# Memory attention and a SiLU feed-forward on one core: weights in order of use, lower parts on GpSimd, folded gates, two buffers for a head's operands

## The chip, the core and the metric

The kernel runs on one core of a Trainium2 chip. The core has a matrix engine (PE, whose weight loads PEld run beside its products), a vector engine (DVE), a scalar engine (ACT), GpSimd (POOL) and a queue, SP, that issues transfers. Each engine takes its instructions in a fixed order, and an instruction that waits holds up everything behind it on that engine. The metric is the device time of one execution in microseconds (us).

## What is computed

```python
# attention with a memory, B=8, H=8, S=576, D=64
scores = where(causal, -1e9, q @ k.T / sqrt(D))
a = exp(scores - scores.max(-1));  a /= a.sum(-1) + 1e-9
local = a @ v
q_p = where(q > 0, q, exp(q) - 1) + 1
mem_out = (q_p @ M_prev) / (q_p @ z_prev + 1e-6)
g = 1 / (1 + exp(-beta))                     # one number per head
x = g * mem_out + (1 - g) * local            # 8*576 tokens x 512
# feed-forward on x: w_in 512 x 2048, w_out 2048 x 512 (given as float64)
h = x @ w_in;  out = (h * sigmoid(h)) @ w_out
```

## The kernel before, in words

**Two kinds of work.** There are 64 heads of attention (8 per batch entry), and a feed-forward of 18 units of 256 tokens, each of 8 steps (p = 0 to 7). A step makes 24 products into a PSUM tile `h` (line 548), turns it into `g` (lines 559 to 564), and makes 12 products into `acc` (line 528). All products but those of the first heads take operands split into a rounded part and a lower part (fp32r), so that a product is made of two or three products at full rate. The first `N_WHOLE` heads take fp32 operands instead ("whole"), which needs no split but more PE time.

**A head** has two generators. `scores` transposes q and k (`tt`), makes the rounded parts (`kk`, `qq`, on ACT) and the lower parts (`kk`, `ql`, `qq`, lines 229 and 232, on DVE), then five blocks of scores: minimum on DVE (260, 291), exponential on ACT with a row sum (262, 296). The last block is laid out as two halves (`pair`) of 64 partitions; one of its halves gets the causal mask by an addition on GpSimd (284). `scale_rows` turns row sums into 1/(sum) on DVE, and GpSimd scales the probabilities by it and by 1 - g (250). `values` transposes the probabilities on PE, splits them (405, 406) and multiplies them with v and the memory (413, 421). `values` of a head runs beside `scores` of the next one.

**Weights** arrive as 64-bit words. `split_weight` decodes one of 32 tiles with two ACT, three DVE and one POOL instructions and splits it with one ACT and one POOL instruction (lines 149 to 161). Twelve of the tiles (`FLOW`) don't stay on chip: they are written to scratch through two `flow` buffers, and read again through the same two buffers in every unit (`flow()`, line 481). In the kernel before, the list `order` holds the twelve FLOW tiles first.

**What sets the order.** The main loop draws steps from three generators: one step of attention, then weights, then feed-forward steps at `FFN_RATE` once `done[0]`, the number of finished heads, is at least 8. `done[0]` counts a head after the next head's `scores` too. From that program a scheduler makes the order of each engine, using buffer counts (`QK_BUFS`, `NB`, `TH_BUFS`, ...) as limits.

Of the kernel before, what the change touches and what calls it, by code (L numbers as in the profile page):

```python
# [34 lines left out]
PREP_FROM = 8  # L35
PREP_REST = 100
# [7 lines left out]
def memory_attention_then_silu_ffn(ctx, tc, q, k, v, M_prev, z_prev, beta, w_in, w_out, out):  # L44
    nc = tc.nc
# [30 lines left out]
    def f(ap):  # L76
# [13 lines left out]
        compare_op=ALU.is_ge, fill=BIG,  # L90
    )
    gate = const.tile([P, H], F32, name="gate")
    omg = const.tile([P, H], F32, name="omg")
    nc.sync.dma_start(out=gate, in_=beta.rearrange("(o h) -> o h", o=1).to_broadcast([P, H]))
    nc.scalar.activation(gate, gate, AF.Exp, scale=-1.0)
    nc.vector.tensor_scalar(gate, gate, 1.0, None, op0=ALU.add)
    nc.vector.reciprocal(gate, gate)
    nc.vector.tensor_scalar(omg, gate, -1.0, 1.0, op0=ALU.mult, op1=ALU.add)
# [41 lines left out]
    def split_weight(kind, c, raw):  # L140
        t = weight_tile(kind, c)
        w = raw
        if raw.dtype == I64:
            words = raw.bitcast(U32).rearrange("p (n t) -> p n t", t=2)
            low, high = words[:, :, 0], words[:, :, 1]
            y = pool.tile([P, DM], U32, tag="wy", name="wy", bufs=W_BUFS)
# [20 lines left out]
    order = [(kind, 2 * p + j) for p in range(NP) for kind in "io" for j in range(2)]  # L167
    order.sort(key=lambda x: x not in FLOW)
# [43 lines left out]
    def scores(b, h, raw, rest, made, whole):  # L212
# [6 lines left out]
        if whole:  # L219
            qq = pool.tile([P, S], F32, tag="kk", name="qf", bufs=QK_BUFS)  # L220
            nc.scalar.activation(qq[0:64], tt[64:P], AF.Copy, scale=QS)
            terms = [(qq[0:64], tt[0:64])]
        else:
            kk = pool.tile([P, S], F32R, tag="kk", name="kk", bufs=QK_BUFS)
            qq = qrow[h % QK_BUFS]
            ql = qlow[h % QK_BUFS]
            nc.scalar.copy(kk[0:64], tt[0:64])
            nc.scalar.activation(qq[64:P, 0:S], tt[64:P], AF.Copy, scale=QS)
            nc.vector.tensor_tensor(out=kk[64:P], in0=tt[0:64], in1=f(kk[0:64]), op=ALU.subtract)
            nc.scalar.activation(qq[0:64, 0:S], tt[64:P], AF.Copy, scale=QS)  # L230
            for low, x0, x1 in ((ql[0:64], 0, S - LAST), (qq[0:64, S:S + LAST], S - LAST, S)):
                nc.vector.scalar_tensor_tensor(
                    out=low, in0=tt[64:P, x0:x1], scalar=QS, in1=f(qq[64:P, x0:x1]),
                    op0=ALU.mult, op1=ALU.subtract)
            nc.scalar.copy(qq[:, S + LAST:], f(qq[:, S - LAST:S]))
            terms = [(qq, kk), (ql, kk)]
# [5 lines left out]

        def scale_rows(n, i0, i1):
            s, r = st[0:n, 10 + i0:10 + i1], st[0:n, 15 + i0:15 + i1]
            nc.vector.tensor_scalar(s, s, 1.0e-9, None, op0=ALU.add)
            nc.vector.reciprocal(r, s)  # L246
            if n == LAST:
                nc.vector.tensor_copy(st[n:P, 15 + i0:15 + i1], r)
            for i in range(i0, i1):
                nc.gpsimd.tensor_scalar(  # L250
                    pb[i], pb[i], st[:, 15 + i:16 + i], omg[:, h:h + 1], op0=ALU.mult, op1=ALU.mult)

        for i in range(NQ - 1):
# [3 lines left out]
            for j, (ta, tb) in enumerate(terms):  # L257
# [3 lines left out]
                s, s, mask[:, 3 * P - P * i:], 1.0, 3.0e38, ALU.add, ALU.min, st[:, i:i + 1]).ins  # L261
# [10 lines left out]
        for side, other, x0, x1, o in ((slice(0, LAST), slice(LAST, P), 0, SPLIT, P),  # L272
                                       (slice(LAST, P), slice(0, LAST), SPLIT, S, 0)):
            s = ps_s.tile([P, 512], F32, tag="s", name="s")[:, 0:x1 - x0]
# [15 lines left out]
        for s, row, more, least in halves:  # L290
            nc.vector.tensor_tensor_reduce(row, s, more, 1.0, 3.0e38, ALU.add, ALU.min, least)
        up, down = slice(0, LAST), slice(LAST, P)
        nc.vector.tensor_copy(st[up, 6:7], st[down, 5:6])
        nc.vector.tensor_tensor(out=st[up, i:i + 1], in0=st[up, 5:6], in1=st[up, 6:7], op=ALU.min)
        anchor["dve"] = nc.vector.tensor_copy(st[down, i:i + 1], st[up, i:i + 1]).ins
        nc.scalar.activation(
            pt, pair, AF.Exp, bias=st[:, i:i + 1], scale=-1.0, accum_out=st[:, 10 + i:11 + i])
        pb.append(pt)
        scale_rows(P, 0, NQ - 1)
        yield  # L300
        nc.vector.tensor_copy(st[up, 7:8], st[down, 10 + i:11 + i])
        nc.vector.tensor_tensor(
            out=st[up, 10 + i:11 + i], in0=st[up, 10 + i:11 + i], in1=st[up, 7:8], op=ALU.add)
        scale_rows(LAST, NQ - 1, NQ)
        if not whole:
            nc.gpsimd.tensor_copy(pt[down, HI:], pt[down, HI - LAST:HI])
# [128 lines left out]
    def attention():  # L435
# [12 lines left out]
        for n in range(len(todo) + 1):  # L448
# [14 lines left out]
            done[0] = n  # L463
# [45 lines left out]
    def ffn():  # L509
        ahead = None  # L510
        for _ in range(FLOW_BUFS):
            flow()
        for u in range(NU):
# [7 lines left out]
            def second(p, g):  # L521
                for c in range(2):
# [8 lines left out]
                    if ("o", 2 * p + c) in FLOW:  # L531
                        flow()

            before = None
            for p in range(NP):
# [6 lines left out]
                for c in range(2):  # L542
# [39 lines left out]
    steps, prepared, produced, steps_made = 0, 0, 0.0, 0
# [48 lines left out]
```

## Time and profile before

| | |
|---|---|
| median of 3 runs | 1349.75 us (1349.42 to 1352.28) |
| profiled execution, its own time | 1345.04 us |
| its span in the profile | 1343.3 us |
| PE busy | 1279.5 us (95%) |
| DVE busy | 1047.2 us (78%) |
| ACT busy | 799.9 us (60%) |
| POOL busy | 661.0 us (49%) |

Busy times are averages over stages that differ: the first heads with the weights (to about 204 us), attention and feed-forward side by side (to about 1140 us), and feed-forward alone. The span is 1.7 us shorter than the execution's own time.

### The profile page before, as it was taken

To read this page: it belongs to the slowest core of one execution; us is meant where nothing else is said; L and a number is where in the kernel's file an instruction comes from. 1 tells how busy PE (TensorE), PEld (TensorE's weight loads), DVE (VectorE), ACT (ScalarE), POOL (GpSimd) and SP (SyncE) were. 2 spreads that over 40 slices of the span, in tenths; PEclk is the share of its full clock that TensorE was granted. 3 is DMA by queue.
4 is the path that set the end of the run, shared out by engine and by line. 5 is a ranking of instruction groups with operands and counts; after the bars stand their busy time and mean duration, and the time that the engine had idled before them with its cause. 6 is when DMAs were issued, how large, how long until landed. Compare 5 with 4: busy or idle time off the path is not lost.

```text
span 1343.3 us, 24742 instructions
## 1 busy us (share of the span) xinstructions
PE 1279.5 (95%) x7863; PEld 1089.2 (81%) x7863; DVE 1047.2 (78%) x2918; ACT 799.9 (60%) x1994; POOL 661.0 (49%) x985
## 2 busy tenths in 40 slices
PE   6999899999999999999899999999999989999998
PEld 2444357998889898989899898989998888899997
DVE  7878996889999889998889888999989888322222
ACT  6766775667667566766666665767766665211111
POOL 5768894555545454555545555555555544111110
PEclk9965799999999999999999999999999999999999
DMA  7865535556455454555454545555555542344444
GB/s 170 233 172 168 138 109 127 150 126 162 123 136 149 119 153 128 146 136 135 130 145 121 160 124 139 146 138 136 150 148 134 136 124 79 126 143 156 157 157 141
DMA packets 302994, 190.39 MB, mean 142 GB/s; under 512 B 258832, under 2 KB 267024, under 8 KB 302864
## 3 DMA queue, kind: packets, MB, share of 16 engines
q1 hardware_dynamic: 302864, 188.82, 51.7%
q8 instruction: 62, 1.02, 0.3%
q14 instruction: 68, 0.56, 0.1%
HBM read 173.02 MB, written 15.73 MB: 141 GB/s over the span
## 4 chain that ended last, share of the span: by engine, by line
PE 68%; DVE 18%; ACT 4%; DMA 3%; POOL 3%; issue 3%; SPq 1%; DVEq 0%; POOLq 0%; ACTq 0%
PE h L548 26%; PE acc L528 22%; PE x L421 7%; PE s L258 5%; PE tp L375 4%; DVE xu L501 1%; DVE th L560 1%; DMA flow<-wo_s 1%; DVE pl L406 1%; DVE tt L218 1%; DVE s L260 1%; DVE qp L358 1%; PE x L413 1%; POOL p L250 1%; DVE e L326 1%
## 5 line engine op out<-in xcount | busy, mean ns | idle before, releaser
L548 PE MATMUL h<-xu,wi 128*128 128x256 f32 x2592 | 381.3, 290 | 30.4 <-DVE th L560 23.1
L548 PEld LDWEIGHTS h<-xu,wi 128*128 128x128 f32 x2592 | 348.6, 195 | 46.6 <-DVE th L560 28.7
L250 POOL TENSOR_SCALAR p<-p,st,omg 128x384 f32<-128x384 f32 (+3 forms) x320 | 232.1, 737 | 109.0 <-DVE st L246 42.4
L528 PE MATMUL acc<-wo,g 128*128 128x512 f32 x864 | 245.6, 400 | 0.5 <-DVE g L564 0.5
L528 PE MATMUL acc<-flow,g 128*128 128x512 f32 x864 | 237.8, 398 | 2.4 <-DMA flow<-wo_s 2.4
L563 POOL TENSOR_SCALAR g<-th 128x512 fp32r<-128x512 f32 x144 | 90.7, 630 | 291.5 <-DVE th L560 269.2
L262 ACT ACTIVATE p<-s,st 128x128 f32<-128x128 f32 (+3 forms) x256 | 134.9, 527 | 125.7 <-DVE st L260 109.6
L560 DVE SCALAR_TENSOR_TENSOR th<-th,h 128x512 f32<-128x512 f32 x144 | 98.4, 684 | 113.6 <-ACT th L559 111.8
L528 PEld LDWEIGHTS acc<-flow,g 128*128 128x128 f32 x864 | 157.1, 188 | 34.5 <-DMA flow<-wo_s 4.1
L528 PEld LDWEIGHTS acc<-wo,g 128*128 128x128 f32 x864 | 151.2, 189 | 22.4 <-DVE g L564 0.9
L559 ACT ACTIVATE th<-h 128x512 f32<-128x512 f32 x144 | 85.2, 592 | 129.9 <-PE h L548 129.5
L260 DVE CUSTOM_DVE_ANT_0 s<-s,mask 128x128 f32<-128x128 f32 (+3 forms) x256 | 123.6, 496 | 21.9 <-PE s L258 20.3
L564 DVE TENSOR_TENSOR g<-th,g 128x512 fp32r<-128x512 f32 x144 | 107.8, 749 | 35.3 <-POOL g L563 33.6
L548 PE MATMUL h<-xu,flow 128*128 128x256 f32 x864 | 130.2, 286 | 0.5 <-DMA flow<-wi_s 0.5
L327 POOL TENSOR_TENSOR r<-e,zb 128x320 f32<-128x320 f32 x64 | 58.2, 910 | 142.5 <-DVE e L326 127.5
L375 PE MATMUL tp<-ident,p 128*128 128x128 f32 x640 | 121.3, 289 | 2.5 <-POOL flow L161 1.5
L406 DVE TENSOR_TENSOR pl<-tp,ph 128x384 fp32r<-128x384 f32 x212 | 114.7, 551 | 9.4 <-ACT ph L405 6.3
L548 PEld LDWEIGHTS h<-xu,flow 128*128 128x128 f32 x864 | 114.3, 191 | 0.9 <-DMA flow<-wi_s 0.7
L405 ACT CAST ph<-tp 128x384 fp32r<-128x384 f32 x212 | 101.2, 490 | 23.1 <-PE tp L383 18.5
L375 PEld LDWEIGHTS tp<-ident,p 128*128 128x128 f32 x640 | 80.1, 146 | 24.9 <-issue 12.2
L421 PE MATMUL x<-ph,vs 128*128 128x320 f32 (+4 forms) x371 | 83.8, 280 | 0.2 <-POOL vs L315 0.2
L421 PE MATMUL x<-pl,vs 128*128 128x320 f32 (+3 forms) x318 | 79.9, 305 | 2.0 <-DVE pl L406 2.0
(106 smaller groups left out, 2346.1 us busy)
## 6 DMA issues: line engine op xcount, KB each, us to landing
flow<-wo_s SPq DMA_DIRECT2D x144, 512.0 KB, 3.5
flow<-wi_s SPq DMA_DIRECT2D x72, 512.0 KB, 4.0
raw<-in_k SPq DMA_DIRECT2D x128, 72.0 KB, 2.9
raw<-in_q SPq DMA_DIRECT2D x128, 72.0 KB, 2.9
out<-o SPq DMA_DIRECT2D x36, 256.0 KB, 4.2
wraw<-in_moe_w_out SPq DMA_DIRECT2D x16, 512.0 KB, 5.2
qn<-in_q SPq DMA_DIRECT2D x64, 128.0 KB, 3.7
vr<-in_v SPq DMA_DIRECT2D x64, 128.0 KB, 3.0
```

Of the source, the lines that this page charges most:

```text
L250: nc.gpsimd.tensor_scalar(pb[i], pb[i], st[:, 15 + i:16 + i], omg[:, h:h + 1], op0=ALU.mult, op1=ALU.mult)
L260: anchor["dve"] = nc.vector.tensor_tensor_reduce(s, s, mask[:, 3 * P - P * i:], 1.0, 3.0e38, ALU.add, ALU.min, st[:, i:i + 1]).ins
L262: nc.scalar.activation(pt, s, AF.Exp, bias=st[:, i:i + 1], scale=-1.0, accum_out=st[:, 10 + i:11 + i])
L375: nc.tensor.transpose(t[:, o:o + P], pb[i][:, P * j:P * j + P], ident)
L405: nc.scalar.copy(ph[:, 0:o], t[:, 0:o])
L406: nc.vector.tensor_tensor(out=pl[:, 0:cut], in0=t[:, 0:cut], in1=f(ph[:, 0:cut]), op=ALU.subtract)
L421: nc.tensor.matmul(x[0:rows, q0:n], vs[0:n_k, j], part[0:n_k, o:o + n - q0], start=False, stop=last)
L528: nc.tensor.matmul(acc[t], ta, tb, start=p == 0 and c == 0 and n == 0, stop=p == NP - 1 and c == 1 and n == len(terms) - 1)
L548: nc.tensor.matmul(h[:, c], ta, tb, start=kk == 0 and n == 0, stop=kk == KD - 1 and n == len(terms) - 1)
L560: nc.vector.scalar_tensor_tensor(out=th, in0=th, scalar=1.0, in1=h, op0=ALU.add, op1=ALU.mult)
L563: nc.gpsimd.tensor_scalar(hi, th, 1.0, 1.0, op0=ALU.mult, op1=ALU.mult)
L564: nc.vector.tensor_tensor(out=lo, in0=th, in1=f(hi), op=ALU.subtract)
```

## The change

Six things change. (1) The list `order` of weights follows their use, resident and FLOW tiles mixed, and they are made at one rate (`PREP_RATE`) instead of 2.5 per nine steps and then all at once. (2) Feed-forward steps may begin as soon as `values` of the eighth head is done, `flow()` waits until its weight is ready, and a step that asks for a weight no longer uses up the allowance of the feed-forward. (3) The lower parts `kk`, `ql`, `qq` go from DVE to GpSimd; the scale of q by -1/8 goes from them into the minimum's instruction. (4) The gates g and 1 - g are folded into the two denominators as `over` (1 + exp(-beta) and 1 + exp(beta)), so that GpSimd scales with one operand column instead of two, and all five scalings of a head come after the last block's sum. (5) `kk`, `qq`, `ql`, `tt` get two buffers; to make room, `th`, `o` and `wy` share four `row` buffers. (6) `N_WHOLE` goes from 11 to 10, so that the eleventh head is split.

```diff
-TH_BUFS = 2
-QK_BUFS = 1
+QK_BUFS = 2
-NB = dict(vs=1, e=2, r=1, qp=1, ms=2, raw=1, qn=2, mr=3, zb=2, st=2, nrm=2, ph=2, pl=2, xb=1, tt=1)
+NB = dict(vs=1, e=2, r=1, qp=1, ms=2, raw=1, qn=2, mr=3, zb=2, st=2, nrm=2, ph=2, pl=2, xb=1, tt=2)
-N_WHOLE = 11
-O_BUFS = 2
-W_BUFS = 4
+N_WHOLE = 10
+ROW_BUFS = 4
-PREP_FLOW = 2.5
-PREP_FROM = 8
-PREP_REST = 100
+PREP_RATE = 3.0
+PREP_AFTER = 3.0
...
+    nc.scalar.activation(bet[:, 0], bet[:, 0], AF.Exp, scale=-1.0)
+    nc.scalar.activation(bet[:, 1], bet[:, 1], AF.Exp)
+    nc.vector.tensor_scalar(bet, bet, 1.0, None, op0=ALU.add)
+    over = const.tile([P, 2, H, NQ], F32, name="over")
+    for j in range(2):
+        for hh in range(H):
+            nc.gpsimd.tensor_scalar(over[:, j, hh], mask[:, 0:NQ], bet[:, j, hh:hh + 1], None, op0=ALU.add)
...
-    order = [(kind, 2 * p + j) for p in range(NP) for kind in "io" for j in range(2)]
-    order.sort(key=lambda x: x not in FLOW)
+    order = [
+        (kind, 2 * x + j) for p in range(NP + 1) for kind, x in (("i", p), ("o", p - 1))
+        if 0 <= x < NP for j in range(2)]
...
-            nc.scalar.activation(qq[64:P, 0:S], tt[64:P], AF.Copy, scale=QS)
-            nc.vector.tensor_tensor(out=kk[64:P], in0=tt[0:64], in1=f(kk[0:64]), op=ALU.subtract)
-            nc.scalar.activation(qq[0:64, 0:S], tt[64:P], AF.Copy, scale=QS)
+            nc.scalar.copy(qq[64:P, 0:S], tt[64:P])
+            nc.gpsimd.tensor_tensor(out=kk[64:P], in0=tt[0:64], in1=f(kk[0:64]), op=ALU.subtract)
+            nc.scalar.copy(qq[0:64, 0:S], tt[64:P])
             for low, x0, x1 in ((ql[0:64], 0, S - LAST), (qq[0:64, S:S + LAST], S - LAST, S)):
-                nc.vector.scalar_tensor_tensor(
-                    out=low, in0=tt[64:P, x0:x1], scalar=QS, in1=f(qq[64:P, x0:x1]),
-                    op0=ALU.mult, op1=ALU.subtract)
+                nc.gpsimd.tensor_tensor(
+                    out=low, in0=tt[64:P, x0:x1], in1=f(qq[64:P, x0:x1]), op=ALU.subtract)
...
-        scale_rows(P, 0, NQ - 1)
         yield
-        nc.vector.tensor_copy(st[up, 7:8], st[down, 10 + i:11 + i])
-        nc.vector.tensor_tensor(
-            out=st[up, 10 + i:11 + i], in0=st[up, 10 + i:11 + i], in1=st[up, 7:8], op=ALU.add)
-        scale_rows(LAST, NQ - 1, NQ)
+        halves_of(10 + i, 6, ALU.add)
+        nc.vector.scalar_tensor_tensor(
+            out=st[:, 15:15 + NQ], in0=st[:, 10:10 + NQ], scalar=1.0e-9, in1=over[:, 1, h],
+            op0=ALU.add, op1=ALU.mult)
+        nc.vector.reciprocal(st[:, 15:15 + NQ], st[:, 15:15 + NQ])
+        for x in range(NQ):
+            nc.gpsimd.tensor_scalar(
+                pb[x], pb[x], st[:, 15 + x:16 + x], 1.0, op0=ALU.mult, op1=ALU.mult)
...
-        nc.vector.tensor_scalar(nrm, nrm, 1.0e-6, None, op0=ALU.add)
+        nc.vector.scalar_tensor_tensor(
+            out=nrm, in0=nrm, scalar=1.0e-6, in1=over[:, 0, h], op0=ALU.add, op1=ALU.mult)
         nc.vector.reciprocal(nrm, nrm)
-        nc.vector.tensor_scalar(nrm, nrm, gate[:, h:h + 1], None, op0=ALU.mult)
...
-                two = two and next(second, "end") != "end"
+                if two and next(second, "end") == "end":
+                    two = False
+                    done[0] = n
...
-            done[0] = n
...
         if flow_order:
+            while flow_order[0] not in ready:
+                yield "prepare"
             x = flow_order.pop(0)
...
-        while going and prepared < 2 * KF and prepared < (
-                PREP_FLOW * min(steps, H * A_STEPS) + PREP_REST * max(steps - PREP_FROM * A_STEPS, 0)) / A_STEPS:
+        started = done[0] >= H
+        while going and len(ready) < min(2 * KF, steps * (PREP_AFTER if started else PREP_RATE) / A_STEPS):
             next(prep)
```

**GpSimd, one head in the middle of the run.** `g` is the feed-forward's rounding, `p_...` are the probabilities, `pair` the mask addition, `r` and `e` the memory's normalization, `vs` and `ms` operands of the values. Before:

```order
L250 TENSOR_SCALAR p_9446<-p_9446,st,omg 128x128
L250 TENSOR_SCALAR p_9488<-p_9488,st,omg 128x256
L250 TENSOR_SCALAR p_9507<-p_9507,st,omg 128x384
L250 TENSOR_SCALAR p_9543<-p_9543,st,omg 128x512
L284 TENSOR_TENSOR pair<-pair,mask 64x64
L317 TENSOR_SCALAR ms<-mr 128x64
L318 TENSOR_TENSOR ms<-mr,ms 128x64
L327 TENSOR_TENSOR r<-e,zb 128x320
L563 TENSOR_SCALAR g<-th 128x512
```

The same engine after the change, from the end of one head's scalings:

```order
L304 TENSOR_SCALAR p_11558<-p_11558,st 128x384
L307 COPY p_11558<-p_11558 64x64
L318 TENSOR_SCALAR ms<-mr 128x64
L319 TENSOR_TENSOR ms<-mr,ms 128x64
L235 TENSOR_TENSOR ql_155<-tt,qq_151 64x512
L235 TENSOR_TENSOR qq_151<-tt,qq_151 64x64
L277 TENSOR_TENSOR pair<-pair,mask 64x64
L328 TENSOR_TENSOR r<-e,zb 128x320
L232 TENSOR_TENSOR kk<-tt,kk 64x576
L315 TENSOR_SCALAR vs<-vr 128x5x64
L316 TENSOR_TENSOR vs<-vr,vs 128x5x64
L567 TENSOR_SCALAR g<-th 128x512
```

The mask addition stood behind four scalings; now it stands behind a row of lower parts, which belong to a later head.

**DVE at the end of a feed-forward unit.** `xu` are the splits of the next unit's tokens, `th` is the instruction that reads `h` last and so frees it for the next unit's products. Before:

```order
L564 TENSOR_TENSOR g<-th,g 128x512
L245 TENSOR_SCALAR st<-st 128x4
L246 RECIPROCAL st<-st 128x4
L406 TENSOR_TENSOR pl<-tp,ph 128x512
L429 TENSOR_TENSOR xt<-x,xb 64x256
L406 TENSOR_TENSOR pl<-tp,ph 128x320
L409 TENSOR_TENSOR ph<-tp,ph 64x64
L291 ISA pair,st<-s,pair 64x256
L291 ISA st 64x1
L232 SCALAR_TENSOR_TENSOR ql_136<-tt,qq_134 64x512
L232 SCALAR_TENSOR_TENSOR qq_134<-tt,qq_134 64x64
L291 ISA pair,st<-s,pair 64x320
```

There follow, up to `th`, `kk` (line 229), the five `xu`, `tt`, `pl`, `qp` and `e`. After the change, the last rows ahead of `th` at the same place:

```order
L430 TENSOR_TENSOR xt<-x,xb 64x256
L284 ISA pair,st<-s,pair 64x256
L284 ISA st 64x1
L505 TENSOR_TENSOR xu<-xt,xu 128x192
L505 TENSOR_TENSOR xu<-xt,xu 128x64
L505 TENSOR_TENSOR xu<-xt,xu 128x192
L505 TENSOR_TENSOR xu<-xt,xu 128x64
L505 TENSOR_TENSOR xu<-xt,xu 128x256
L564 SCALAR_TENSOR_TENSOR th<-th,h 128x512
```

The lower parts have left this stretch, and here the half of `pair` that waits for GpSimd has moved behind `th`; in units 8 to 13 of the 18 it still stands ahead of it.

**SP at the start of the feed-forward.** `wi_s`, `wo_s` are the scratch copies. Before, the first read of a FLOW weight stands behind the writes of eleven of the twelve, and the twelfth follows two rows later:

```order
L137 DMA wraw<-in_moe_w_out 128x512
L481 DMA flow<-wi_s_101 128x1024
L208 DMA zb<-in_z_prev 128x64
L163 DMA wo_s_129<-flow 128x1024
L206 DMA mr<-in_M_prev 64x64 x2
```

After, the first read stands behind the loads (`raw`) of the thirteenth head instead of the eighth, and reads and the last writes alternate:

```order
L164 DMA wi_s_129<-flow 128x1024
L201 DMA qn_146<-in_q 128x4x64
L202 DMA qn_146<-in_q 64x64
L204 DMA vr<-in_v 128x4x64
L485 DMA flow<-wi_s_117 128x1024
L164 DMA wo_s_143<-flow 128x1024
L206 DMA vr<-in_v 64x64 x2
L193 DMA raw<-in_k 32x18x32 x2
L193 DMA raw<-in_q 32x18x32 x2
L211 DMA zb<-in_z_prev 128x64
L485 DMA flow<-wo_s_131 128x1024
```

With two buffers for both, a read has now to wait for a write two places ahead of it, and the last weight for a read's use.

## Rows read from the trace of the kernel before

**Rows 1.** The page's first part: busy time, share of the span and instructions.

```profile
PE 1279.5 (95%) x7863; PEld 1089.2 (81%) x7863; DVE 1047.2 (78%) x2918; ACT 799.9 (60%) x1994; POOL 661.0 (49%) x985
```

**Rows 2.** Windows: stretch, length, busy us (instructions) per engine, granted clock, DMA share, GB/s.

```profile
84.00:130.00 46.00, 42.88 (x108) 19.71 (x108) 34.03 (x89) 30.11 (x72) 35.98 (x33) 0.50 0.59 152
165.00:204.00 39.00, 36.18 (x167) 21.84 (x167) 36.65 (x79) 26.08 (x62) 37.16 (x32) 0.93 0.38 99
...
816.00:918.00 102.00, 100.19 (x684) 92.58 (x683) 91.41 (x278) 70.06 (x180) 54.00 (x90) 1.00 0.53 142
...
1020.00:1120.00 100.00, 93.99 (x626) 85.68 (x624) 86.63 (x253) 65.98 (x167) 50.78 (x85) 0.98 0.46 125
...
1140.00:1335.00 195.00, 193.71 (x1240) 175.79 (x1239) 57.40 (x95) 32.82 (x67) 22.21 (x36) 1.00 0.45 148
```

**Rows 3.** Waits from 240 to 1130 us: total us, times, longest.

```profile
PE h L548 <- DVE th L560: 22.8, 17, 4.4
PE s L258 <- DVE kk L229: 1.6, 1, 1.6
```

**Rows 4.** Chain that ended last, 655 to 675 us: start, us, what.

```profile
663.82 2.44 POOL p L250 x3
...
666.56 0.33 POOL pair L284
...
670.24 1.33 DVE xu L501 x2
671.58 0.61 DVE th L560
```

**Rows 5.** Timeline of PE, the four longest stops at L548; idle time in brackets.

```profile
460.98 4.62 PE L548 MATMUL h<-xu,wi 128*128 128x256 f32 x24 [2.61 <-DVE th L560]
...
672.23 4.63 PE L548 MATMUL h<-xu,wi 128*128 128x256 f32 x24 [3.50 <-DVE th L560]
...
811.21 4.43 PE L548 MATMUL h<-xu,wi 128*128 128x256 f32 x24 [2.07 <-DVE th L560]
...
1088.89 4.63 PE L548 MATMUL h<-xu,wi 128*128 128x256 f32 x24 [4.36 <-DVE th L560]
```

**Rows 6.** A window of 3.4 us right behind a stop of Rows 5.

```profile
672.60:676.00 3.40, 3.40 (x19) 3.40 (x18) 3.21 (x11) 1.39 (x6) 1.22 (x2) 0.50 0.94 216
```

**Rows 7.** DVE groups, 240 to 1130 us: busy us, mean ns, idle before.

```profile
L232 DVE SCALAR_TENSOR_TENSOR ql<-tt,qq 64x512 fp32r<-64x512 f32 x51 | 39.9, 783 | 4.0 <-ACT qq L228 2.5
L229 DVE TENSOR_TENSOR kk<-tt,kk 64x576 fp32r<-64x576 f32 x51 | 39.7, 779 | 4.7 <-ACT kk L227 3.3
L232 DVE SCALAR_TENSOR_TENSOR qq<-tt,qq 64x64 fp32r<-64x64 f32 x51 | 13.1, 256 | 0.2
```

**Rows 8.** POOL groups, 240 to 1130 us, and DVE's wait for one of them.

```profile
L563 POOL TENSOR_SCALAR g<-th 128x512 fp32r<-128x512 f32 x103 | 65.2, 633 | 110.8 <-DVE th L560 88.4 <-DVE st L245 11.8 <-DVE nrm L332 3.9
L315 POOL TENSOR_TENSOR vs<-vr,vs 128x320 fp32r<-128x320 f32 x51 | 45.1, 884 | 2.9
L250 POOL TENSOR_SCALAR p<-p,st,omg 128x512 f32<-128x512 f32 x51 | 44.0, 863 | 0.0
L284 POOL TENSOR_TENSOR pair<-pair,mask 64x64 f32<-64x64 f32 x51 | 19.2, 376 | 15.7 <-ACT pair L282 11.9 <-PE tq L350 1.1
...
DVE pair L291 <- POOL pair L284: 19.2, 35, 2.5
```

**Rows 9.** The DVE group of the folded gate g, 0 to 204 us.

```profile
L332 DVE TENSOR_SCALAR nrm<-nrm,gate 128x5 f32<-128x5 f32 x11 | 5.0, 453 | 0.1
```

**Rows 10.** The page's transfers: KB each, median us from issue to landing.

```profile
flow<-wo_s SPq DMA_DIRECT2D x144, 512.0 KB, 3.5
```

**Rows 11.** Timeline of PE at full clock: score products, whole and split.

```profile
175.95 1.77 PE L258 MATMUL s<-tt,qf 64*128 64x384 f32 x4
...
258.38 0.39 PE L258 MATMUL s<-kk,qq 128*128 128x512 f32 x1
258.61 0.39 PE L258 MATMUL s<-kk,ql 128*128 128x512 f32 x1
```

More of the change, by code (lines that the diff above doesn't have):

```diff
@@ L89, in memory_attention_then_silu_ffn @@
         out=mask[:, 3 * P:], in_=mask[:, 3 * P:], pattern=[[-1, P]], base=0, channel_multiplier=1,
-        compare_op=ALU.is_ge, fill=BIG,
+        compare_op=ALU.is_ge, fill=BIG / QS,
     )
[L92 to L98, printed above, removed]
+    bet = pool.tile([P, 2, H], F32, tag="st", name="bet", bufs=NB["st"])
+    nc.sync.dma_start(out=bet[:, 0], in_=beta.rearrange("(o h) -> o h", o=1).to_broadcast([P, H]))
+    nc.vector.tensor_copy(bet[:, 1], bet[:, 0])
+    nc.scalar.activation(bet[:, 0], bet[:, 0], AF.Exp, scale=-1.0)
[5 more added lines that the diff above has]
+            nc.gpsimd.tensor_scalar(over[:, j, hh], mask[:, 0:NQ], bet[:, j, hh:hh + 1], None, op0=ALU.add)
     weight, scratch = {}, {}
@@ L145, in split_weight @@
             low, high = words[:, :, 0], words[:, :, 1]
-            y = pool.tile([P, DM], U32, tag="wy", name="wy", bufs=W_BUFS)
+            y = pool.tile([P, DM], U32, tag="row", name="wy", bufs=ROW_BUFS)
             w = f(y)
@@ L220, in scores @@
             qq = pool.tile([P, S], F32, tag="kk", name="qf", bufs=QK_BUFS)
-            nc.scalar.activation(qq[0:64], tt[64:P], AF.Copy, scale=QS)
+            nc.scalar.copy(qq[0:64], tt[64:P])
             terms = [(qq[0:64], tt[0:64])]
@@ L241, in scores @@
         pb = []
[L243 to L251, printed above, removed]
         for i in range(NQ - 1):
@@ L260, in scores @@
             anchor["dve"] = nc.vector.tensor_tensor_reduce(
-                s, s, mask[:, 3 * P - P * i:], 1.0, 3.0e38, ALU.add, ALU.min, st[:, i:i + 1]).ins
+                s, s, mask[:, 3 * P - P * i:], QS, 3.0e38, ALU.add, ALU.min, st[:, i:i + 1]).ins
             nc.scalar.activation(
@@ L273, in scores @@
                                        (slice(LAST, P), slice(0, LAST), SPLIT, S, 0)):
-            s = ps_s.tile([P, 512], F32, tag="s", name="s")[:, 0:x1 - x0]
+            s = ps_s.tile([P, 512], F32, tag="s", name="s")
+            s = s[:, 0:x1 - x0]
             row = pair[side, o:o + x1 - x0]
@@ L511, in ffn @@
         for _ in range(FLOW_BUFS):
-            flow()
+            yield from flow()
         for u in range(NU):
@@ L531, in second @@
                     if ("o", 2 * p + c) in FLOW:
-                        flow()
+                        yield from flow()
             before = None
@@ L551, in ffn @@
                     if ("i", 2 * p + c) in FLOW:
-                        flow()
+                        yield from flow()
                 yield
                 if before:
-                    second(*before)
+                    yield from second(*before)
                 h = h.rearrange("p c t -> p (c t)")
-                th = pool.tile([P, 2 * T], F32, tag="th", name="th", bufs=TH_BUFS)
+                th = pool.tile([P, 2 * T], F32, tag="row", name="th", bufs=ROW_BUFS)
                 nc.scalar.activation(th, h, AF.Tanh, scale=0.5)
@@ L570, in ffn @@
                 yield
-            second(*before)
+            yield from second(*before)
             for t in range(T // P):
-                o = pool.tile([P, DM], F32, tag="o", name="o", bufs=O_BUFS)
+                o = pool.tile([P, DM], F32, tag="row", name="o", bufs=ROW_BUFS)
                 nc.scalar.activation(o, acc[t], AF.Copy, scale=0.5)
@@ L581, in memory_attention_then_silu_ffn @@
     att, prep, prod = attention(), preparation(), ffn()
[L582 removed]
+    steps, produced, steps_made = 0, 0.0, 0
     going = True
@@ L586, in memory_attention_then_silu_ffn @@
         steps += 1
-        while going and prepared < 2 * KF and prepared < (
-                PREP_FLOW * min(steps, H * A_STEPS) + PREP_REST * max(steps - PREP_FROM * A_STEPS, 0)) / A_STEPS:
+        started = done[0] >= H
+        while going and len(ready) < min(2 * KF, steps * (PREP_AFTER if started else PREP_RATE) / A_STEPS):
             next(prep)
-            prepared += 1
-        if done[0] >= H:
+        if started:
             produced += (FFN_RATE if steps_made >= FIRST_UNITS * F_STEPS else FIRST_RATE) * F_STEPS / A_STEPS
@@ L599, in memory_attention_then_silu_ffn @@
                 next(prep)
-                prepared += 1
+                continue
             produced -= 1.0
-            steps_made += said != "prepare"
+            steps_made += 1
     for _ in prep:
```

14 lines of the change are left out of this document (8 added, 6 removed).

## The prediction

> **What bounds the kernel now.** I read the page's first part, then windows by stage, then the waits of PE, then the chain at the places where PE stops. By the page PE is the fullest engine, 95% of the span [rows 1], but the windows show three stages with different limits [rows 2]. In the last stage, from about 1140 us, PE runs 1240 products in 195 us at full clock and is busy all the time; the orders of before and after leave about 1,210 feed-forward products behind the last attention product in both, so nothing is to be won there. In the middle, 102 us hold 684 products where PE doesn't stop, and 100 us hold 626 where it does. [...]
>
> In the middle PE waits mainly for one thing: `th` on DVE, which frees the single PSUM tile `h`, 22.8 us in 17 waits [rows 3]. The chain says why it is late [rows 4]: four scalings of probabilities on POOL hold up the mask addition (`pair`), DVE stands still until that is done, then clears its queue, `xu` of the next unit's tokens among it, and only then comes to `th`. The four longest stops are 2.61, 3.50, 2.07 and 4.36 us [rows 5]. After such a stop the granted clock is 0.50 for 3.4 us [rows 6]; that is 1.7 us lost each.
>
> **The change, part by part.** My sum is made against the profiled execution, 1345.04 us; the median of the runs, 1349.75, lies 4.7 us above it, and I add that at the end.
>
> *Lower parts off DVE.* Each split head loses 783 + 779 + 256 ns = 1.82 us of DVE [rows 7]. This DVE time is on no path by itself, only where it stands between the last products of a unit and `th`. There, before, all three parts stand ahead of `th` in nearly every unit, and after the change none does. So each stop can shrink by 1.82 us at most: the four long ones give 4 x 1.82 = 7.3 us, the other thirteen (22.8 - 12.5 = 10.3 us, 0.8 us each on average) could go altogether. The cap is 17.6 us. The floor is nothing, since DVE still waits for `pair` ahead of `th` in units 8 to 13. I take 13. With the long stops shortened to 0.3 to 2.5 us the drops of the clock should mostly go too: four of them are 6.8 us, I take 4 (bounds 0 and 6.8).
>
> *The same parts on POOL.* The trace has no such part on POOL. Its two-input subtraction costs 884 ns for 320 columns and the addition of 64 columns 376 ns [rows 8], 1.98 ns a column between them. By that 576, 512 and 64 columns cost 1.39, 1.27 and 0.38 us, 3.0 us a head. [...] POOL has room: 54.0 of 102 us busy [rows 2], and with 51 heads in 890 us [rows 7] a head takes 17.5 us, of which POOL works 9.3. With 3.0 more, less what the scalings give back (below), that is 64 to 70%.
>
> What is queued behind the new work matters more. The five scalings of a head now stand in one piece (before, four and one), and `pair`, the feed-forward's `g` and the lower parts of a later head behind one another. `g` was already waited for through DVE, and `pair` costs DVE 19.2 us in 35 waits [rows 8]. I add 3 us for new waits that reach PE; below, nothing, because two buffers let the lower parts be made a head ahead; above, 40 us, the first rival.
>
> *Folded gates.* Per head DVE loses three small scalar instructions (lines 245, 330 and 332) and gets two that take a tile as second operand. Line 332 takes 453 ns on average in the first stage [rows 9]; I take the net of one such instruction, 0.45 us a head, 4.5 us over the first ten heads if DVE set their pace throughout (bounds 0 and 9, if the new ones cost half). It does so only towards 204 us. GpSimd's scaling takes 863 ns with two columns; the nearest row with none, `g`, takes 633 for the same shape [rows 8], so a head's five scalings may lose between 0 and 1.1 us, of POOL time that nothing waits for except in the same last part of the first stage. The sixteen small instructions that make `over` stand at the start, where POOL has no other work yet.
>
> *Weights and the earlier start.* All 32 weights cost what they did. In the orders PE's first products of a feed-forward step with `acc` move up by one head, but by the eleventh head the number of products done is the same (101 and 36 before, 96 and 36 after), so the earlier start by itself is worth nothing. Against it stands the SP queue, where reads of FLOW weights now alternate with the last writes. Cover for that is attention's own products between the feed-forward's; if it is too short, a read takes 3.5 us to land [rows 10]. For the whole first stage (gates, scalings, smoother weights, two buffers) I take 4 us. The lower bound is a loss of 7, two such reads; the upper bound is 15: the 4.5 us of DVE, and 10 us in case the clock stays up from 84 to 130 us, where DVE and POOL would be the next limit with 34 and 36 of 46 us.
>
> *The eleventh head split.* A whole head's two large score products, 896 columns, take 1.77 us, 1.98 ns a column; split products are issued 0.23 us apart for 512 columns, 0.45 ns a column [rows 11]. By the code a whole head has 1856 + 2176 = 4032 columns of scores and values, a split one 3136 + 3712 = 6848; that is 8.0 against 3.1 us, a gain of 4.9 us of PE in a stretch where PE is 36.2 of 39 us busy [rows 2]. I take 4 (bounds 0 and 5); its price on the other engines is counted above.
>
> Sum: 13 + 4 + 4 + 4 - 3 = 22 us. 1345.0 - 22 = 1323, and on the runs' level 1327.7; I say **1328 us**.
>
> **The rivals.**
>
> *POOL comes late for the scores (slower).* POOL makes `kk` last of the lower parts; if the five scalings and `g` ahead of it are late, PE's first score product stops, and the feed-forward behind it on PE too. Before, PE waited for `kk` only once, 1.6 us [rows 3], with the part on a DVE that is 90% full. Speaking for it: POOL works in long pieces now, about 3.5 us for five scalings and 3.0 for the parts. Against it: the two buffers. One wait of the length of `kk`, 1.39 us, at every second of 54 heads is 37 us: 1365 us. It decides from 22/54 = 0.4 us a head. [...]
>
> *The stops stay.* The change does not reach `th`: `pair` and `g` now stand behind other work on POOL, and DVE waits as long as before. Then 13 + 4 fall away but for a few us: about 1342 us. For it speaks that the releaser in the chain is POOL [rows 4], whose load grows; against it that `xu` and the lower parts are DVE's own 3 us of that delay.
>
> [...]
>
> **How the numbers follow.** The forecast gets 0.55 (its own range 1317 to 1338), POOL late 0.15, stops that stay 0.20, the clock 0.10. The range 1305 to 1346 takes in the second and most of the third and leaves out the slower rival. A measurement of this kernel tells about 0.2%, 2.7 us. Faster: 0.55 + 0.10 + 0.14 of the stops that stay = 0.79; within 0.2%: 0.06; slower 0.15.
>
> **What would show it.** Right: PE's waits at `h` for `th` from 240 us on fall from 22.8 to under 12 us, the half-clock windows behind them mostly vanish, DVE in the middle falls from 90 to about 75% and POOL rises to 64 to 70%; the three parts on POOL take 3.0 us together; the last attention product comes some 20 us sooner and the rest after it takes as long as before. Wrong: a new wait of `s` or `tp` for POOL in the list of waits that sums to more than 20 us; stops at `th` of the old size, with POOL's `pair` or `g` ahead in the chain; or PE stopped for FLOW reads between 165 and 230 us.

## The result and the profile after

The changed kernel takes 1336.79 us (median of 4 runs, 1331.87 to 1338.53) against 1349.99 us of the kernel before beside it: a ratio of 0.9901 [0.988, 0.9922], 13.2 us faster. The profiled executions differ by as much, 1331.87 against 1345.04 us (spans 1330.1 and 1343.3 us). The forecast was 1328. The changed kernel's profiled execution is the fastest of its four and lies 4.9 us below their median, so differences between single profiled executions carry some 5 us of spread.

The page's first part, which answers to [rows 1]: DVE has lost 84 us of busy time and POOL gained 137.

```profile
PE 1269.9 (95%) x7858; PEld 1084.7 (82%) x7858; DVE 963.4 (72%) x2580; ACT 805.2 (61%) x1999; POOL 798.1 (60%) x1169
```

Windows with the stretches of [rows 2], and two longer ones. From 84 to 130 us the granted clock is 0.70, no longer 0.50; in the middle DVE is less full and POOL fuller.

```profile
84.00:130.00 46.00, 37.47 (x113) 18.21 (x114) 40.31 (x93) 34.79 (x82) 39.82 (x37) 0.70 0.68 189
165.00:204.00 39.00, 34.38 (x181) 22.88 (x182) 32.26 (x69) 26.70 (x68) 37.52 (x42) 0.96 0.60 154
816.00:918.00 102.00, 98.58 (x659) 90.98 (x660) 79.56 (x229) 65.97 (x168) 64.83 (x104) 0.98 0.49 133
1020.00:1120.00 100.00, 96.89 (x662) 88.58 (x661) 78.53 (x218) 62.48 (x158) 60.13 (x101) 1.00 0.38 118
...
0.00:240.00 240.00, 208.19 (x796) 115.78 (x797) 193.49 (x465) 168.55 (x405) 192.58 (x213) 0.89 0.62 166
240.00:1130.00 890.00, 866.33 (x5828) 792.37 (x5828) 715.36 (x2027) 604.76 (x1531) 583.04 (x922) 1.00 0.50 135
```

The same two long windows of the kernel before:

```profile
0.00:240.00 240.00, 209.92 (x753) 109.79 (x754) 192.27 (x487) 160.66 (x388) 176.04 (x177) 0.83 0.61 160
240.00:1130.00 890.00, 861.48 (x5788) 791.16 (x5787) 791.19 (x2314) 601.30 (x1528) 457.65 (x764) 0.99 0.52 136
```

The products are the same ones but for five fewer in the eleventh head (7858 and 7863 recorded), so they place the gain. At 240 us the changed kernel has 7858 - 796 = 7062 products left and takes 1090.1 us for them, 6.48 a us; the kernel before has 7110 left. The 48 more are 7.4 us; the other 5.8 us are gained behind 240 us. Some 7 us come from the first stage, then, and some 6 from behind it.

PE's waits from 240 to 1130 us, which answer to [rows 3] (total us, times, longest):

```profile
PE h L552 <- DVE th L564: 6.5, 10, 1.6
PE tp L376 <- DVE qp L359: 3.7, 2, 2.9
PE s L250 <- ACT p L254: 3.6, 4, 2.3
PE s L250 <- DVE st L284: 2.0, 2, 1.0
PE s L274 <- ACT p L254: 1.8, 2, 1.2
PE tp L376 <- DVE pl L407: 1.5, 4, 0.5
PE x L422 <- ACT ph L406: 1.1, 2, 0.5
```

The stops at `h` for `th` fell from 22.8 us [rows 3] to 6.5, by 16.3. But all other stops, 5.5 us before, are now 16.8 (those shown and six more of under 1 us each): 11.3 us of the 16.3 came back at other places. POOL is the releaser named in none of them.

POOL's groups from 240 to 1130 us (busy us, mean ns, idle before), which answer to [rows 8]: kk and ql took 1.45 and 1.36 us. With 0.35 for the 64 columns of qq the three parts are 3.2 us a head. The scaling of 512 columns costs 709 ns, before 863.

```profile
L232 POOL TENSOR_TENSOR kk<-tt,kk 64x576 fp32r<-64x576 f32 x50 | 72.7, 1453 | 4.3 <-ACT kk L230 0.5
L235 POOL TENSOR_TENSOR ql<-tt,qq 64x512 fp32r<-64x512 f32 x50 | 68.0, 1361 | 15.0 <-ACT qq L231 11.3 <-POOL vs L316 0.9 <-POOL g L567 0.2
L304 POOL TENSOR_SCALAR p<-p,st 128x512 f32<-128x512 f32 x52 | 36.9, 709 | 0.0
```

The longest new stop, 2.87 us, in the timelines of DVE, POOL and PE:

```profile
867.17 1.07 POOL L316 TENSOR_TENSOR vs<-vr,vs 128x320 fp32r<-128x320 f32 x1
...
867.42 0.84 DVE L331 SCALAR_TENSOR_TENSOR nrm<-nrm,over 128x5 f32<-128x5 f32 x1
868.29 0.43 DVE L359 TENSOR_TENSOR qp<-tq,qp 64x256 fp32r<-64x256 f32 x1
...
868.86 0.52 PE L376 MATMUL tp<-ident,p 128*128 128x128 f32 x3 [2.87 <-DVE qp L359]
```

PE waits for `qp` on DVE, and `qp` stands behind line 331. That instruction has 5 columns; it takes 0.15 us at the least, here 0.84, and it ends at 868.26 us, within 0.02 us of POOL's subtraction (868.24). This accounts for 0.7 of the 2.87 us. The subtraction is `vs`, which POOL made before the change too. The same is seen where POOL makes a lower part:

```profile
544.29 1.94 POOL L232 TENSOR_TENSOR kk<-tt,kk 64x576 fp32r<-64x576 f32 x1
...
544.86 1.39 DVE L290 TENSOR_TENSOR st<-st 64x1 f32<-64x1 f32 x1
...
791.37 1.29 POOL L235 TENSOR_TENSOR ql<-tt,qq 64x512 fp32r<-64x512 f32 x1 [0.38 <-ACT qq L231]
...
791.84 0.84 DVE L331 SCALAR_TENSOR_TENSOR nrm<-nrm,over 128x5 f32<-128x5 f32 x1
```

Line 290 works on one column and takes 1.39 us: it ends 0.02 us after `kk` on POOL. Line 331 ends 0.02 us after `ql`. These are not single cases. Of the 128 instructions of line 290, 39 take more than 0.3 us, and each of them ends within 0.02 us of the end of a POOL instruction; so do, within 0.04 us, the 36 of line 331's 64 that take more than 0.3 us. In 66 of these 75 POOL's instruction has two inputs, in 40 it is `kk` or `ql`. Where line 290 meets no POOL instruction, it takes 0.11 to 0.15 us; no short one of either line lies within a two-input POOL instruction, four lie within one with one input. So the long instructions of these two lines, with two operands each, lasted to the end of a two-input POOL instruction in 66 cases and of one with a single input in 9; what makes them last is not shown.

Two operands were not needed for it: in the kernel before, the `TENSOR_SCALAR` of lines 245 (four columns) and 330, with one tile as operand, take more than 0.3 us in 12 and 18 of 64 cases, and each of these ends within 0.04 us of the end of a POOL instruction. The changed kernel's 128 copies of line 289 are not lengthened: 148 to 151 ns, also the 52 that lie within a two-input POOL instruction.

### The profile page after: what moved, and what is told of

It is laid out like the page before. It is cut to its first block, busy times and chain, and to the rows that moved or that the text cites. A ratio compares the mean times of both kernels' runs of the same rounds, so it can differ in the third digit from the quotient of the medians.

```text
span 1330.1 us, 24649 instructions
## 1 busy us (share of the span) xinstructions
PE 1269.9 (95%) x7858; PEld 1084.7 (82%) x7858; DVE 963.4 (72%) x2580; ACT 805.2 (61%) x1999; POOL 798.1 (60%) x1169
## 4 chain that ended last, share of the span: by engine, by line
PE 71%; DVE 13%; ACT 6%; DMA 4%; issue 3%; POOL 2%; SPq 1%; DVEq 0%; POOLq 0%; ACTq 0%
PE h L552 27%; PE acc L532 24%; PE x L422 7%; PE s L250 5%; PE tp L376 4%; DVE s L252 2%; PE x L414 1%; PE tq L351 1%; DMA zb<-in_z_prev 1%; DVE xu L505 1%; DMA flow<-wo_s 1%; DVE th L564 1%; DVE wy L152 1%; DVE wy L159 1%; ACT p L254 1%
## 5 line engine op out<-in xcount | busy, mean ns | idle before, releaser
L552 PE MATMUL h<-xu,wi 128*128 128x256 f32 x2592 | 373.8, 287 | 10.0 <-DVE th L564 7.3
L552 PEld LDWEIGHTS h<-xu,wi 128*128 128x128 f32 x2592 | 342.6, 191 | 24.9 <-DVE th L564 5.9
L304 POOL TENSOR_SCALAR p<-p,st 128x384 f32<-128x384 f32 (+3 forms) x320 | 186.1, 600 | 127.4 <-DVE st L302 121.2
L532 PE MATMUL acc<-flow,g 128*128 128x512 f32 x864 | 230.9, 395 | 0.7 <-DMA flow<-wo_s 0.7
L407 DVE TENSOR_TENSOR pl<-tp,ph 128x384 fp32r<-128x384 f32 x216 | 118.4, 550 | 38.1 <-ACT ph L406 33.9
L568 DVE TENSOR_TENSOR g<-th,g 128x512 fp32r<-128x512 f32 x144 | 104.8, 728 | 50.5 <-POOL g L567 49.3
L552 PE MATMUL h<-xu,flow 128*128 128x256 f32 x864 | 126.7, 284 | 0.0
L406 ACT CAST ph<-tp 128x384 fp32r<-128x384 f32 x216 | 104.7, 490 | 23.6 <-PE x L422 14.7
L235 POOL TENSOR_TENSOR ql<-tt,qq 64x512 fp32r<-64x512 f32 x54 | 73.2, 1356 | 20.6 <-ACT qq L231 11.3
L422 PE MATMUL x<-pl,vs 128*128 128x256 f32 x324 | 81.7, 307 | 0.0
```

The source lines that it names most:

```text
L304: nc.gpsimd.tensor_scalar(pb[x], pb[x], st[:, 15 + x:16 + x], 1.0, op0=ALU.mult, op1=ALU.mult)
L406: nc.scalar.copy(ph[:, 0:o], t[:, 0:o])
L407: nc.vector.tensor_tensor(out=pl[:, 0:cut], in0=t[:, 0:cut], in1=f(ph[:, 0:cut]), op=ALU.subtract)
L422: nc.tensor.matmul(x[0:rows, q0:n], vs[0:n_k, j], part[0:n_k, o:o + n - q0], start=False, stop=last)
L532: nc.tensor.matmul(acc[t], ta, tb, start=p == 0 and c == 0 and n == 0, stop=p == NP - 1 and c == 1 and n == len(terms) - 1)
L552: nc.tensor.matmul(h[:, c], ta, tb, start=kk == 0 and n == 0, stop=kk == KD - 1 and n == len(terms) - 1)
```

## The experiments

Each experiment was timed beside the kernel before; differences from the changed kernel are taken between the ratios. The last two columns compare the profiled execution with that of the changed kernel (span 1330.1 us): what it has lost by 240 us (products left beyond the changed kernel's 7062, at 6.48 a us) and what behind it. They carry the spread of single executions: a_f221, as fast as the changed kernel by its median, stands at 4.6 us in them.

| kernel | median, us | before, us | ratio [95%] | lost by 240 us | behind |
|---|---|---|---|---|---|
| changed kernel | 1336.79 | 1349.99 | 0.9901 [0.988, 0.9922] | - | - |
| a_f221 | 1336.57 | 1348.52 | 0.9912 [0.9883, 0.994] | 2.3 | 2.3 |
| a_whole11 | 1339.67 | 1346.6 | 0.9945 [0.9921, 0.9969] | 2.8 | 3.1 |
| a_two_col | 1346.6 | 1347.18 | 1.0 [0.9983, 1.0017] | 10.0 | 4.5 |
| a_lower_dve | 1353.34 | 1346.6 | 1.0046 [1.0026, 1.0067] | 7.4 | 17.1 |
| a_whole9 | 1353.7 | 1347.18 | 1.0048 [1.0031, 1.0065] | 7.6 | 18.7 |
| a_one_buf | 1355.39 | 1346.6 | 1.0065 [1.0043, 1.0086] | 12.5 | 9.5 |
| a_old_start | 1358.51 | 1348.95 | 1.0072 [1.0054, 1.0089] | 17.3 | 7.7 |
| a_kk_dve | 1363.07 | 1347.18 | 1.0122 [1.0107, 1.0137] | 6.2 | 25.6 |
| b_pool_two | 1380.86 | 1348.95 | 1.0241 [1.0218, 1.0263] | 25.5 | 22.1 |
| a_old_gates | 1384.97 | 1348.95 | 1.0282 [1.0252, 1.0311] | 23.3 | 28.4 |
| a_pool_twice | 1405.53 | 1348.95 | 1.0415 [1.0392, 1.0439] | -0.6 | 75.8 |
| b_lower_pool | 1402.78 | 1346.6 | 1.0422 [1.039, 1.0454] | 5.9 | 63.0 |

**a_lower_dve.**

```diff
-            nc.gpsimd.tensor_tensor(out=kk[64:P], in0=tt[0:64], in1=f(kk[0:64]), op=ALU.subtract)
+            nc.vector.tensor_tensor(out=kk[64:P], in0=tt[0:64], in1=f(kk[0:64]), op=ALU.subtract)
...
-                nc.gpsimd.tensor_tensor(
+                nc.vector.tensor_tensor(
```

> The changed kernel with one thing undone: the three lower parts of a head (kk, ql, qq) are subtracted on VectorE again. Theory M (the gain comes from the lower parts leaving VectorE): the stops of TensorE at h for th come back to 17 to 23 us between 240 and 1130 us, the time rises by 8 to 13 us to 1345 to 1350 us. Theory F (the gain comes from the first stage: weights, gates, eleventh head): the time rises by less than 4 us, to at most 1341 us.

0.0145 x 1346.6 = 19.5 us slower than the changed kernel, more than theory M's 8 to 13, and even slower than the kernel before. The stops for `th` came back to 11.9 us only (16 times), not to 17:

```profile
PE h L552 <- DVE th L564: 11.9, 16, 1.7
...
240.00:1130.00 890.00, 860.02 (x5701) 782.62 (x5701) 785.70 (x2175) 598.79 (x1530) 441.57 (x770) 0.98 0.50 134
```

All other stops of PE in this stretch sum to 16.8 us, as many as in the changed kernel. So of the 17.1 us lost behind 240 us the stops hold only 5.4. Most of the rest is the granted clock: it is 0.50 for 27.2 us of the stretch, in the changed kernel for 6.8; half of the difference is some 10 us of PE's time, an estimate.

The second measurement is in DVE's groups, here of this kernel and then of the changed one:

```profile
L290 DVE TENSOR_TENSOR st<-st 64x1 f32<-64x1 f32 x128 | 28.0, 219 | 2.2
L331 DVE SCALAR_TENSOR_TENSOR nrm<-nrm,over 128x5 f32<-128x5 f32 x64 | 21.1, 330 | 1.0
```

```profile
L290 DVE TENSOR_TENSOR st<-st 64x1 f32<-64x1 f32 x128 | 43.1, 337 | 1.4
L331 DVE SCALAR_TENSOR_TENSOR nrm<-nrm,over 128x5 f32<-128x5 f32 x64 | 29.5, 461 | 1.2
```

With the parts on DVE they take 54 x (819 + 801 + 269 ns) = 102.0 us there, yet DVE's busy time is only 1040.9 - 963.4 = 77.5 us higher. So 24.5 us of what the move takes off DVE comes back as longer DVE instructions, 15.1 and 8.4 of it in these two lines.

**b_lower_pool**: the kernel before with `gpsimd` for the three parts, and

```diff
-                s, s, mask[:, 3 * P - P * i:], 1.0, 3.0e38, ALU.add, ALU.min, st[:, i:i + 1]).ins
+                s, s, mask[:, 3 * P - P * i:], QS, 3.0e38, ALU.add, ALU.min, st[:, i:i + 1]).ins
```

> The kernel before with one part of the change alone: the three lower parts on GpSimd (with the scale taken in the mask addition instead, as the part needs it), one buffer for the operands as before. Theory M: th's stops fall from 22.8 to under 10 us and the time falls by 6 to 13 us, to 1337 to 1344 us, unless the single buffer puts GpSimd's parts in front of the scores; then new stops of s for kk or tp appear and the time is 1350 us or more. Theory F: within 4 us of 1350.

57 us slower than before (0.0422 x 1346.6), although the stops for `th` halve, 22.8 to 11.1 us. The part alone is as slow as the forecast's slower rival, and slower, but not by the rival's wait: PE's new stops are spread over `acc` for FLOW reads (8.4 us), `s` for ACT's `p` (6.1), `x` for ACT's `ph` (5.8), and only 2.3 us name POOL's `kk`:

```profile
PE s L257 <- POOL kk L229: 2.3, 2, 1.7
```

DVE's wait for `pair` on POOL rises from 19.2 [rows 8] to 39.4 us.

**a_one_buf**: `QK_BUFS = 1` and `tt=1`.

> The changed kernel with one buffer each for tt, kk, qq and ql, as before. If the second buffers are what keeps GpSimd's lower parts off the path (the forecast's reason against its slower rival), TensorE waits for kk or ql at the scores in many heads and the time rises by 10 to 37 us, to 1347 to 1374 us. If GpSimd's slack alone does it, less than 4 us, at most 1341 us.

22 us slower (0.0164 x 1346.6). Buffers are needed, but not for the reason given: only two stops, 2.6 us, name `kk` in the middle, and more than half of the profiled execution's loss, 12.5 of 22.0 us, lies before 240 us, where the first ten heads are whole and have no lower parts. There the transposed `tt` and the copy of q have one buffer each; that these are what costs the time is likely, not shown.

**a_whole11**: `N_WHOLE = 11`, and **a_whole9**: `N_WHOLE = 9`.

> The changed kernel with the eleventh head whole again (N_WHOLE 11). The forecast's own term (4 us, bounds 0 to 5): 1341 us. Theory F, which puts most of the 13 us into the first stage, would allow up to 1345; if TensorE is not what the first stage waits for there, no change, 1337 us.

> The changed kernel with one whole head fewer (N_WHOLE 9): the tenth head is split too. If TensorE's time in the first stage is still what counts, another 5 to 6 us faster, 0.985 to 0.987 of before, the same step as from eleven to ten. If GpSimd, which takes 3.2 us more for a split head and is 37.5 of 39 us busy from 165 to 204 us, has become the limit there, no gain or a loss, 0.990 or more.

The eleventh head is worth 0.0044 x 1346.6 = 5.9 us, with both intervals between 2 and 10; I had 4. The tenth costs 20 us instead of saving 5. The profiled execution, 26.3 us behind the changed kernel's and the slowest of its six, has lost 18.7 of them behind 240 us, where it does what the changed kernel does, in another order: PE's stops there sum to 31.0 us instead of 23.3, and the granted clock is 0.50 for 23.8 us instead of 6.8. So an order alone can be worth some 10 us, even with the spread of the two profiled executions taken off.

**a_f221**: `FFN_RATE = 0.221`.

> A control without any part of the change undone: the changed kernel with the pace of the feed-forward steps raised by half a per cent (FFN_RATE 0.221 for 0.22). Every instruction is the same; TensorE's order is the same for its first 824 of some 3,360 rows, to about the fifteenth head, and is another one after that. If the 20 to 50 us that undoing single parts cost are the prices of those parts, this one stays at the changed kernel, 0.988 to 0.992 of before. If a good share of them is only that any edit makes another order out of the program, and the changed kernel has a lucky one, this one is slower too, 0.996 or more.

1.5 us from the changed kernel, inside the interval: this other order costs nothing. With a_whole9 it limits what single undone parts tell: a difference of some 20 us (a_lower_dve, a_one_buf, a_old_start) may be the order in good part, and 50 us were seen only with a part behind them. The expectation asked for one or the other; two kernels don't settle how often an order costs that much.

**b_pool_two**: b_lower_pool with `QK_BUFS = 2`, `tt=2`, and `wy`, `th` and `o` in one ring of four. **a_old_gates**: the changed kernel with `gate`, `omg` and `scale_rows` of before.

> The kernel before with two parts of the change together and nothing else: the lower parts on GpSimd and two buffers for a head's operands (wy, th and o share a ring of four to make room, as in the change). Theory P (parts and buffers only work together, and are most of the gain): well under 1402.8 us, and faster than before, 1333 to 1342 us. Theory G (the gates folded into one scaling pass are needed too, since the scalings in two pieces stand between GpSimd's parts): slower than before, 1352 to 1385 us.

> The changed kernel with the gates as before (a second column in the scalings, four scaled early and one late, three small instructions per head on VectorE). Theory P: small, 0 to 5 us slower than the changed kernel, which stands at 0.990 of before, so at most 1339 us beside a before of 1347. Theory G: 10 us or more slower, with VectorE's wait for GpSimd's pair, 9.1 us after the change, back at 19 us or above.

Theory P falls: parts and buffers without the folded gates are 32.5 us slower than before, and the old gates cost the changed kernel 51 us (0.0381 x 1349), the dearest part to undo. DVE is 51.9 us busier with them (1015.3 against 963.4 us, 0.81 us a head; I had 0.45); beside the parts on POOL the small instructions of lines 330 and 332 last longer, 492 and 437 ns on average, in the kernel before 273 and 294. DVE's wait for `pair` is 12.4 us, not 19: that mark of theory G did not show. PE's largest stop is another:

```profile
PE tp L381 <- DVE pl L412: 13.6, 18, 1.3
```

**a_two_col**: the scalings with a second column, and nothing else.

```diff
-                pb[x], pb[x], st[:, 15 + x:16 + x], 1.0, op0=ALU.mult, op1=ALU.mult)
+                pb[x], pb[x], st[:, 15 + x:16 + x], one, op0=ALU.mult, op1=ALU.mult)
```

> The changed kernel with a column of ones as the second factor of each probability scaling on GpSimd, where it now has a constant: the same result, the same place in the program, and the duration of before (863 instead of about 720 ns for 512 columns, some 0.6 us more of GpSimd a head). It splits the 51 us that the old gates cost. If it is GpSimd's time, at the slope of the doubled parts (70 us for 3.2 us a head) it is 13 us slower than the changed kernel, 1.000 of before; if the price of the old gates is mostly this time, 1.02 or more; if it is mostly that the fifth scaling waits for a second round through VectorE, under 1.004.

13.3 us slower (0.0099 x 1347), for 28.0 us more of POOL's time (826.1 against 798.1); 512 columns take 797 ns on average over the whole run, in the changed kernel 719. The 13 us of the expectation came out, but that is no proof of its reason: 10.0 of the 14.5 us that the profiled execution loses lie before 240 us, where the doubled parts below lose nothing. The other 38 of the 51 us hang on where the scalings stand, on DVE's three more instructions a head and on the order; which of them was not separated.

**a_old_start**: `order`, the rates and the place of `done[0] = n` as before.

> The changed kernel with the old order and pace of the weights and the old start of the products (weights that are read back first, 2.5 a head, then the rest at once after eight heads). If the smoother start is worth the 7 us by which the changed kernel has fewer products left at 240 us, 5 to 8 us slower, at 0.994 to 0.996 of before. If that lead comes from the second buffers and the eleventh head, as the forecast's zero for the earlier start says, within 3 us of the changed kernel, at 0.988 to 0.992.

23 us slower (0.0171 x 1349); the profiled execution loses 17.3 of its 25.0 us by 240 us. The windows where the last weights are decoded in a burst, to be held against the changed kernel's 181 products from 165 to 204 us:

```profile
165.00:204.00 39.00, 28.39 (x101) 15.33 (x100) 30.32 (x63) 28.83 (x70) 38.15 (x39) 0.75 0.49 111
204.00:240.00 36.00, 28.95 (x178) 26.65 (x179) 22.31 (x56) 15.53 (x38) 19.97 (x30) 0.86 0.35 97
```

POOL is full, and PE makes 101 products; the kernel before, with the same burst but no lower parts on POOL, had POOL nearly as full (37.16 of 39 us) and made 167 [rows 2].

**a_pool_twice**: the three subtractions issued twice. **a_kk_dve**: `kk` alone on DVE.

> The changed kernel with GpSimd making each of the three lower parts twice (3.2 us more of its time a head, the result the same). It measures how near the slower rival is. If GpSimd has slack at the scores, as its 67% busy time in the middle suggests, under 8 us slower (0.990 to 0.996 of before). If its parts are already nearly late, each head waits for a good part of the 3.2 us: 54 heads, half of them waiting, 80 us slower, 1.05 of before.

> The changed kernel with one of the three lower parts, kk, on VectorE again (0.78 us a head there, 1.46 less on GpSimd). If what limits the middle is GpSimd's share of a head alone, faster than the changed kernel by the slope of the doubled parts, up to 30 us: 0.97 to 0.985 of before. If it is VectorE's as well, and the change stands near the balance, between the changed kernel and the one with all three parts on VectorE: 0.990 to 1.005.

Doubling costs 69 us (0.0514 x 1349): 1.3 us a head for 3.2 us of POOL, though POOL is busy 69% of the span. Line 290's instruction (294 there) is longer again, 486 ns, after 219 with no part on POOL and 337 with one set:

```profile
L294 DVE TENSOR_TENSOR st<-st 64x1 f32<-64x1 f32 x128 | 62.2, 486 | 2.3
```

With `kk` back on DVE the time is not between its two neighbours: 30 us slower than the changed kernel (0.0221 x 1347), 10 slower than with all three back. PE waits 8.5 us for `th` and 4.2 for line 290. Why half a move is worse than either end stays open. No kernel here beats the changed one.

## Why the forecast was right in sign and 9 us too low

*The stops at `h`.* Right in size: 13 us forecast, 16.3 recovered (cap 17.6), and the rival "stops stay" is out. The forecast gave all of it to the lower parts, and that is only in part so. Taken back to DVE they return 5.4 of the 16.3 us (a_lower_dve); moved alone they take away 11.7 (b_lower_pool). The rest comes with the other edits or the order that they make, so the size is luck in part.

*The clock.* Two half-speed stretches of 3.4 us are left in the middle (granted clock 0.53 in both windows), where there were four (0.50 to 0.51); at 1.7 us each that is 3.4 us, I had 4. a_f221, as fast by its median, has four in its profile, so the term is no better known than that. One stands behind the stop that `qp` makes:

```profile
869.90:873.30 3.40, 3.40 (x19) 3.40 (x18) 3.31 (x10) 1.50 (x5) 0.98 (x2) 0.53 0.48 88
```

*The new waits.* This is the term that failed: "I add 3 us for new waits that reach PE". They are 11.3 us (a_f221: 19.3 us of other stops instead of 5.5, so 13.8), and not in the form that I looked for. I looked for PE waiting for POOL, and for work queued behind POOL's pieces; the profile names DVE or ACT. One way is DVE's lengthened instructions, above: at the longest stop that is 0.7 of 2.87 us. But most of the 11.3 us can't be laid to the parts on POOL, since a_lower_dve, with the parts on DVE, has the same 16.8 us of other stops. What makes them stays open; they come with the other edits or with the order.

In the middle, then, 16.3 us of stops and 3.4 of the clock were won and 11.3 lost, 8.4 in all. Behind 240 us 5.8 were gained: the last stage takes 1.1 back, and 1.5 are not placed. The forecast had 13 + 4 - 3 = 14.

*DVE and POOL.* DVE in the middle fell to 715.4 of 890 us, 80%, and not to 75. The 51 heads x 1.82 us of the forecast lead from 791.2 to 698.4 us, 78%; the 17.0 us above that are less than the 24.5 us by which a_lower_dve shows DVE's instructions lengthened over the whole run. POOL, at 66%, came out as forecast.

*The three parts on POOL.* 3.2 us a head for 3.0.

*The first stage and the eleventh head.* 8 us forecast, 7.4 measured at 240 us. Behind this sum the parts are not confirmed. a_whole11 has 2.8 us of the eleventh head's price by 240 us, 5.9 by its median. The earlier start and the smoother weights, "worth nothing" and part of a term of 4, cost 23 us when undone, and the gates, for which I counted DVE's time, 51; my terms hold neither. I read line 332's 453 ns as its own cost, but of its 11 instructions there the five that end with no POOL instruction take 0.22 to 0.23 us, and the six that end within 0.03 us of the end of one 0.37 to 0.92: half of the mean is the lengthening. So that the sum came near is partly luck. The case of a clock that stays up, given 0.10, was my estimate, and its 10 us no run shows: the granted clock from 84 to 130 us is 0.70 instead of 0.50, but PE makes 113 products there instead of 108.

*The slower rival.* It was given 0.15, with the two buffers as the reason against it. b_lower_pool, b_pool_two and a_pool_twice are slower by 32 to 69 us, so its price was near; its wait, PE's for `kk` at the scores, is 2.3 us in the first and none in the other two, so its mechanism was not seen. Without the buffers, the smooth weights or the folded gates the changed kernel is slower than before, too; through which waits was not shown. In the kernel before, the move to GpSimd loses 57 us; in the changed kernel the measurement decides for GpSimd, by 19.5 us, of which the order may be a good part.

*The last product* comes 14.3 us sooner (1146.6 to 1132.3 us), not 20, and the rest after it takes as long, within 1.1 us.

## What to carry to other kernels

Before work moves from DVE to POOL, list DVE's small instructions, those with two operands first, and ask what waits behind each: in the changed kernel 75 of the 192 of one and five columns on lines 290 and 331 took 0.30 to 1.42 us, where those that met no POOL instruction took 0.11 to 0.17, and ended with a POOL instruction. A term for POOL's queue alone misses this. Don't price the parts of a tuned change one by one and add: here a gain of 13 us holds parts that cost 20 to 50 us each when taken out, and the move that carries the idea loses 57 us alone. Count a stop of PE with the stretch at a granted clock of 0.50 that may follow it: in a_lower_dve the added stretches cost some 10 us and the added stops 5. To say what a part is worth, run a control that only changes the order: one gave 1.5 us, another kernel's profiled execution lost 18.7 us in a stretch where its work was the same.

## What the hardware showed that was not expected

DVE's small instructions that end with POOL's, above: 24.5 us of DVE time for 54 heads, most of it in instructions of one and five columns.

The granted clock did not tell PE's rate near the start. Eight equal products in the changed kernel, and in a_lower_dve, whose orders are alike up to the tenth head:

```profile
63.29 3.44 PE L422 MATMUL x<-ph,vr 128*64 128x320 f32 x8
77.43 1.87 PE L422 MATMUL x<-ph,vr 128*64 128x320 f32 x8
```

```profile
84.74 3.44 PE L422 MATMUL x<-ph,vr 128*64 128x320 f32 x8
```

The 3.44 us are 1.84 times the 1.87, while the granted clock reads 1.00 in the windows of all three (60 to 68 and 76 to 80 us, in a_lower_dve 84 to 88). In the one execution the rate rises at about 68 us, in the other at about 89, with the same instructions: the fourth head's `tq` starts at 79.2 and at 88.1 us. So the 7.4 us that a_lower_dve has lost by 240 us are probably not the price of the lower parts. The rise is as late in a_whole9 and a_kk_dve (fourth `tq` at 88.0 and 88.2 us) and as early in a_whole11, a_f221 and a_pool_twice (77.8 to 78.7), all with the same start. What decides when the rate rises was not found.
